# A third bank in the output projection, values of the second block by 7 products, and attention moved to the borders between groups

## The chip, the cores and the metric

One core of a Trainium2 chip. The metric is device time in microseconds (us) of one execution; lower is better. Executions of one kernel in one session agree within a few tenths of a per cent (0.7 at most here, in head_only). The experiments ran on three chips; each timed ratio compares a kernel with the one before on the same chip in the same rounds, while traces are compared across chips. The time of a run is mostly about 1.8 us longer than the span of its cores; both are quoted, and never mixed in one difference.

## The reference

Eight batches of attention with keys and values projected to 64 rows, then one gated feed-forward layer over all 8192 tokens:

```python
k_proj = np.einsum('ks,bhsd->bhkd', E, k)          # 8 batches, 8 heads, 1024 x 64
v_proj = np.einsum('ks,bhsd->bhkd', F, v)
scores = np.matmul(q, k_proj.transpose(0, 1, 3, 2)) / np.sqrt(64)
attn = exp(scores - max); attn /= attn.sum(-1)     # shortened
x = np.matmul(attn, v_proj)                        # then 8192 tokens x 512
gate = 1.0 / (1.0 + np.exp(-(x @ w_gate)))         # 512 -> 1536
val = x @ w_val
return (gate * val) @ w_out                        # 1536 -> 512
```

## The kernel before

The tokens go in 16 blocks of 512, two to a batch. In a block TensorE makes 12 gate tiles (4 matmuls of 128x512 each), 12 value tiles and an output projection, and between these the attention of the next batch. From the third block on, the values are made by 7 products of half-size matrices in place of 8 (a Strassen-type scheme: sums of inputs and of weights are formed on VectorE first, and products are combined in the banks of PSUM, the memory that matmuls write, and by adds afterwards). Matmuls then have 256 columns, and 28 of them replace 16 of 512. From the second block on, the output projection works in the same way. The first two blocks take their values plainly:

```python
for blk in (0, 1):
    todo.append(lambda blk=blk: first_pair(blk, None if blk else lambda: xo(1)))
    for m in range(2, NF):
        todo.append(lambda blk=blk, m=m: mstep(blk, m))    # 4 gate + 4 value matmuls, 512 columns
for tt in range(4):
    todo.append(lambda tt=tt: oproj(0, tt, ffn.next()))
# ... attention(1) hung on slots 12 to 22, weight sums on slot 13
```

One group of four value tiles by 7 products. `A11` to `A22` are quarters of the input, `B11` to `B22` of the weights, `S` and `T` sums of them. TensorE takes a gate tile between any two of these pieces; `v_snap` is a copy on ScalarE, `v_add` and `hidden` run on VectorE:

```python
def p1():
    held_v["a"] = a = FF.take()
    v_product(blk, q, a, "A11", "B11", start=True)              # product 1
    v_snap(0, a)
def p26():
    a = held_v["a"]
    held_v["c"] = c = FF.take()
    v_product(blk, q, c, "A12", "B21", start=True, stop=True)   # product 2
    v_add(0, c)
    v_product(blk, q, a, "S2", "T2")                            # product 6, needs weight sum 2
    v_snap(1, a)
    hidden(K, 0, 0, vsnap[0][:, :], [("vsnap", 0)])
def p57():
    a, c = held_v["a"], held_v["c"]
    v_product(blk, q, c, "S1", "T1", start=True)                # product 5, needs v_add(0) done
    v_product(blk, q, a, "S3", "T3")
    v_snap(2, a)
    v_add(2, c)
# ... p4 (A22 T4) and p3 (S4 B22) finish the group
```

The output projection, cut to the order that matters; `keep_snap` runs on ScalarE, `add_snap`, `plus` and `s_sums` on VectorE:

```python
def first_products(blk, hooks={}):
    a, c = AA.two()
    product(blk, a, "A11", "B11", True)
    keep_snap(0, a)
    product(blk, c, "A12", "B21", True, True)
    hooks.get(-1, int)()                        # in the sixth batch a multiplication of the attention
    add_snap(0, c, 0, 0)                        # frees c
    ...
    product(blk, a, "S2", "T2")
    product(blk, c, "S1", "T1", True)           # waits for that add

def final_products(blk):
    ...
    plus(snap[1], [("snap", 1)], 1, c, slice(0, 512))
    product(blk, b, "A12", "B21", True, True)
    add_snap(0, b, 0, 0)
    s_sums(blk, 4, (0, 6))                      # last product waits for this sum
```

Each engine's instructions run in the order of the program text, and the program waits on semaphores where data need it. So a slot in the schedule decides what stands in front of an instruction in its engine's queue.

The softmax here doesn't subtract the row's maximum and nothing guards it: scores larger than these inputs give would overflow.

## Time and profile before

| | before |
|---|---|
| time, median of the first three runs (range) | 533.45 us (533.1 to 534.06) |
| span of the trace | 531.77 us |
| first gate tile of the first block starts | 21.10 us |
| first gate tile of the second block ("the border") | 45.46 us |
| first product of the second block's projection | 87.00 us |
| from there to the end | 444.77 us |

In the lines of the profile PE is TensorE, PEld its weight loads, DVE VectorE, ACT ScalarE, POOL GpSimd and SP SyncE.

The change adds three groups, in a stretch where the engines are used like this (columns: stretch and length, busy time and count of TensorE, weight loads, VectorE, ScalarE, GpSimd, clock, DMA share, GB/s):

```profile
45.00:87.00 42.00, 41.07 (x267) 17.77 (x270) 27.32 (x44) 20.05 (x38) 3.65 (x4) 1.00 1.21 197
```

VectorE is idle for a third of this stretch (27.3 of 42 us), which is what invites the change.

### The profile page before, as it was taken

The numbers are of one execution on the slowest core, as the hardware profiler recorded it, in microseconds if no ns is written. First come the engines' busy times: TensorE is split into PE (matmuls) and PEld (weight loads), VectorE is DVE, ScalarE is ACT, GpSimd is POOL, SyncE is SP. The second block draws the span as 40 slices with busy tenths as digits, with TensorE's granted clock in tenths as the row PEclk, the third lists the DMA queues.
The fourth block names the chain that finished last, engine by engine and source line by source line (L and its number), as shares of the span: only waits on it lengthen the run. The fifth ranks groups of instructions, "written<-read, shape, count | busy, mean of one in ns | idle before, by whom it ended". The sixth has DMA issues, their size and how long they took to land.

```text
span 531.8 us, 10315 instructions
## 1 busy us (share of the span) xinstructions
PE 515.8 (97%) x4074; PEld 347.1 (65%) x4137; DVE 407.9 (77%) x662; ACT 302.8 (57%) x544; POOL 133.6 (25%) x148
## 2 busy tenths in 40 slices
PE   4999999999999999999999999999999999999997
PEld 4544446656857667585766767676685867777676
DVE  3645386888987788877988679887888788897855
ACT  2654733588385574846568474764838564554541
POOL 9310200105800085001930048100650009200000
DMA  9999999893294254911689224962520020202022
GB/s 158 200 198 203 164 201 217 144 192 75 37 222 78 81 92 66 235 40 61 91 145 173 80 46 48 209 109 80 92 80 1 1 82 3 79 2 80 1 80 80
DMA packets 77152, 56.18 MB, mean 106 GB/s; under 512 B 34800, under 2 KB 69296, under 8 KB 77104
## 3 DMA queue, kind: packets, MB, share of 16 engines
q0 software_dynamic: 33984, 29.89, 36.4%
q1 hardware_dynamic: 43120, 25.63, 19.7%
q8 instruction: 32, 0.52, 0.4%
q14 instruction: 16, 0.13, 0.1%
HBM read 60.29 MB, written 16.78 MB: 145 GB/s over the span
## 4 chain that ended last, share of the span: by engine, by line
PE 91%; DMA 4%; DVE 3%; issue 1%; POOL 1%; ACT 0%; DVEq 0%; ACTq 0%; POOLq 0%
PE pF L264 60%; PE pA L264 30%; DMA KVs<-in_v_dram 2%; DMA qT<-Qb 2%; DVE xT L952 1%; DVE hT L1153 0%; DVE rden L844 0%; POOL KVs L282 0%; POOL Qb L282 0%; DVE ost L1283 0%; DVE vsnap L1489 0%; DVE xT L691 0%; DVE rden L639 0%; DVE hT L1231 0%; DVE EF L1353 0%
## 5 line engine op out<-in xcount | busy, mean ns | idle before, releaser
L264 PE MATMUL pF<-xT,wG 128*128 128x512 bf16 x709 | 187.7, 379 | 4.0 <-issue 0.4
L920 POOL PARTITION_BROADCAST KVs<-eT x96 | 97.0, 1037 | 244.6 <-PE pF L264 191.8
L268 ACT ACTIVATE sig<-pF 128x512 f32<-128x512 f32 x192 | 115.5, 602 | 52.9 <-PE pF L264 50.9
L1489 DVE TENSOR_TENSOR vsnap<-pF,vsnap 128x512 f32<-128x512 f32 x126 | 86.8, 689 | 38.5 <-PE pF L264 28.8
L264 PEld LDWEIGHTS pF<-xT,wG 128*128 128x128 bf16 x768 | 73.7, 98 | 57.6 <-issue 1.7
L268 ACT ACTIVATE vsnap<-pF 128x512 f32<-128x512 f32 x126 | 75.3, 598 | 45.0 <-PE pF L264 42.3
L1470 DVE SCALAR_TENSOR_TENSOR hT<-sig,vsnap 128x512 bf16<-128x512 f32 x126 | 87.3, 693 | 6.2 <-ACT vsnap L268 0.5
L264 PE MATMUL pF<-xT,wV 128*128 128x256 bf16 (+1 forms) x429 | 75.4, 296 | 0.2
L264 PE MATMUL pA<-wO,hT 128*128 128x256 bf16 x534 | 63.4, 273 | 0.4 <-DVE hT L1231 0.4
L264 PEld LDWEIGHTS pF<-xT,wV 128*128 128x128 bf16 x432 | 40.7, 98 | 27.7 <-issue 5.3
L264 PEld LDWEIGHTS pA<-wO,hT 128*128 128x128 bf16 x534 | 52.2, 98 | 7.0 <-DVE hT L1231 0.7
L264 PE MATMUL pF<-xS,wV 128*128 128x256 bf16 x336 | 50.5, 273 | 0.3 <-DVE vsnap L1489 0.2
L264 PE MATMUL pF<-xS,vT 128*128 128x256 bf16 x336 | 50.4, 273 | 0.0
L952 DVE TENSOR_TENSOR xT<-xu,KVs 128x512 bf16<-128x512 f32 x48 | 47.4, 1023 | 1.2 <-POOL KVs L920 0.7
L264 PEld LDWEIGHTS pF<-xS,wV 128*128 128x128 bf16 x336 | 32.2, 98 | 23.7 <-DVE vsnap L1489 3.9
L268 ACT ACTIVATE EF<-pA 128x512 f32<-128x512 f32 x30 | 17.9, 597 | 47.9 <-PE pA L264 47.9
L264 PE MATMUL pA<-wT,hT 128*128 128x256 bf16 x360 | 44.2, 273 | 0.0
L264 PE MATMUL pA<-wT,hS 128*128 128x256 bf16 x360 | 41.9, 273 | 0.6 <-DVE ost L1283 0.6
L264 PEld LDWEIGHTS pA<-wT,hT 128*128 128x128 bf16 x360 | 35.2, 98 | 7.1
L264 PEld LDWEIGHTS pA<-wT,hS 128*128 128x128 bf16 x360 | 35.1, 98 | 4.9 <-DVE ost L1283 0.9
L264 PEld LDWEIGHTS pF<-xS,vT 128*128 128x128 bf16 x336 | 32.9, 98 | 3.8
L1283 DVE SCALAR_TENSOR_TENSOR ost<-pA,EF 128x512 f32<-128x512 f32 x29 | 20.0, 689 | 19.3 <-PE pA L264 19.1
(112 smaller groups left out, 487.7 us busy)
## 6 DMA issues: line engine op xcount, KB each, us to landing
out_dram<-ost SPq DMA_DIRECT2D x60, 256.0 KB, 2.4
Qb<-in_q_dram POOLq DMA_DIRECT2D x7, 1024.0 KB, 20.2
KVs<-in_k_dram POOLq DMA_DIRECT2D x7, 1024.0 KB, 12.6
KVs<-in_v_dram POOLq DMA_DIRECT2D x7, 1024.0 KB, 16.4
wO<-in_moe_w_out_dram POOLq DMA_DIRECT2D x1, 1536.0 KB, 12.3
wG<-in_moe_w_gate_dram POOLq DMA_DIRECT2D x5, 256.0 KB, 18.5
wV<-in_moe_w_val_dram POOLq DMA_DIRECT2D x5, 256.0 KB, 19.0
KVs<-in_k_dram POOLq DMA_DIRECT2D x2, 512.0 KB, 8.4
```

Source lines behind the costliest of these rows:

```text
L264: return add("PE", lambda e: e.matmul(o, lhsT, rhs, **kw), r=r, x=[("bank", b)])
L268: return add("ACT", lambda e: e.activation(o, i, func, scale=scale), r=r, w=w, x=x)
L920: lambda e, n=n, i=2 * rnd + c, j=j, parts=parts: e.partition_broadcast(rb[0:parts, n, :], rrow[32 * j : 32 * j + 1, i, :], channels=parts),
L952: lambda e: e.tensor_tensor(xT[s][:, r, :, 256 * g : 256 * g + 256], xu[:, n, :].rearrange("p (f c) -> p f c", f=2), y.rearrange("p (f c) ...
L1283: lambda e: e.scalar_tensor_tensor(o, bank[bk][:, :].rearrange("p (j c) -> p j c", j=2), 0.5, snap[n].rearrange("p (j c) -> p j c", j=2), ...
L1470: lambda e: e.scalar_tensor_tensor(o, sg[:, :, cc], 1.0, x.rearrange("p (j c) -> p j c", j=2), ALU.add, ALU.mult,),
L1489: lambda e: e.tensor_tensor(o, bank[bk][:, :], o, ALU.add),
```

## The change

The intent is to take columns off TensorE (the second block's values by 7 products in place of 8) and to remove waits (a third PSUM bank in the projection, so that no product waits for the first add; an earlier sum in the last block). To make room, the second batch's attention moves to the borders between groups, the first batch's second half moves one tile earlier, and a few constants move to other memory so that the weight sums can be written sooner. The diff, cut to its core:

```diff
 def first_products(blk, hooks={}):
-    a, c = AA.two()
+    a, c, d = AA.take(), AA.take(), AA.take()
     ...
-    product(blk, c, "A12", "B21", True, True)
+    product(blk, d, "A12", "B21", True, True)
     hooks.get(-1, int)()
-    add_snap(0, c, 0, 0)
+    add_snap(0, d, 0, 0)
+    AA.append(d)
 # --- final_products
-    plus(snap[1], [("snap", 1)], 1, c, slice(0, 512))
     product(blk, b, "A12", "B21", True, True)
+    s_sums(blk, 4, (0, 6))
     add_snap(0, b, 0, 0)
-    s_sums(blk, 4, (0, 6))
+    plus(snap[1], [("snap", 1)], 1, c, slice(0, 512))
 # --- the schedule of the first two blocks
-put(13, lambda: (vt_sums(3), vt_sums(2)))
+put(9, lambda: vt_sums(3))
+put(9, x_sums(1, 1, 2))
+put(10, lambda: (vt_sums(2), vt_sums(1)))
+for u in range(3):                              # second block: three groups of 7 products
+    pieces, p3 = quad_pieces(3 + u, u < 2)
+    todo += [last_piece] + pieces
+    last_piece = p3
+on(0, 1, x_sums(1, 3, 4))
+on(0, 2, lambda: vt_sums(4))
+on(0, 6, n1["k_alone"])                         # attention of the second batch
+on(1, 4, n1["v_alone"])
+for u, name in ((2, "scores"), (3, "mixed")):
+    on(u, 0, n1[name])
 ...
```

`on(u, j, ...)` hangs work behind piece j of group u, `put(i, ...)` behind tile i.

More of the change, by code (lines that the diff above doesn't have):

```diff
@@ L144, in bass_linformer_attn__then__ffn_glu_sigmoid_kernel @@
         vT = sbuf("vT", [P, 3, 2, DFF // 2], BF16)
-        early = vT[:, :, :, :].rearrange("p a b c -> p (a b c)")
+        wT = sbuf("wT", [P, 4, NF // 2, 256], BF16)
+        early = [vT[:, :, :, :].rearrange("p a b c -> p (a b c)")]
         used = [0]
@@ L154, in within @@
                 n *= 2
-            t = early[:, used[0] : used[0] + n]
+            t = early[0][:, used[0] : used[0] + n]
             used[0] += n
@@ L168, in bass_linformer_attn__then__ffn_glu_sigmoid_kernel @@
         bsel8f = within([P, 4, 2, 64], FP32)
-        used[0] = 2 * DFF
+        early[0], used[0] = wT[:, :, :, :].rearrange("p a b c -> p (a b c)"), 0
         bsel8 = within([P, 4, 2, 64], BF16)
@@ L210, in bass_linformer_attn__then__ffn_glu_sigmoid_kernel @@
         ost = sbuf("ost", [P, 4, DM], FP32)
-        wT = sbuf("wT", [P, 4, NF // 2, 256], BF16)
         hS = sbuf("hS", [P, 2, NF // 2, 256], BF16)
@@ L805, in k_alone @@
             def k_alone():
-                bk = att.next()
+                bk = AA.take()
                 project(0, 0, [bk, bk], 0)
                 keep_k(bk, 0)
+                AA.append(bk)
             def v_alone():
-                bk = att.next()
+                bk = AA.take()
+                turn_k(Ring((bk,)))
+                AA.append(bk)
+                bk = AA.take()
                 project(1, 1, [bk, bk], 0)
                 keep_v([bk, bk], 0, ["ACT"] * 4)
+                AA.append(bk)
             def sc_one(r, bks):
@@ L885, in bc @@
             def bc(rnd):
-                bks = [att.next() for _ in range(4)]
+                bks = [AA.take() for _ in range(4)]
                 for half_ in range(2):
@@ L900, in bc @@
                     mul(n // 2, n % 2, bks[j])
+                    AA.append(bks[j])
             def gather():
@@ L971, in two @@
                 return [ring.next(), ring.next()]
-            def scores():
-                f, a0, a1 = two(ffn), two(att), two(att)
-                order = (0, 1, 2)
-                for r, bks in zip(order, (f, a0, a1)):
-                    sc_one(r, bks)
-                exp_one(order[0], f)
-                exp_one(order[1], a0)
-                held["sc"] = a1
-            def mixed():
-                f, a0, a1 = two(ffn), two(att), two(att)
-                sc_one(3, f)
-                xo_one(0, a0)
-                xo_one(1, a1)
-                exp_one(3, f)
-                keep_x(0, a0)
-                held["x"] = a1
-            def outputs():
-                f, a0 = two(ffn), two(att)
-                xo_one(2, f)
-                xo_one(3, a0)
-                held["x"] = a0
-                den8(att.next())
-                keep_x(2, f)
-                rec(0)
-            if b == 1:
-                return [
-                    k_alone,
-                    lambda: (turn_k(att), v_alone()),
-                    scores,
-                    lambda: exp_one(2, held["sc"]),
-                    mixed,
-                    lambda: keep_x(1, held["x"]),
-                    outputs,
-                    lambda: rec(1),
-                    lambda: (keep_x(3, held["x"]), split()),
-                    lambda: bc(0),
-                    lambda: bc(1),
-                ]
             def exp_half(r, g, bks):
@@ L1063, in outputs3 @@
                 xo_one(3, a0)
+                if b == 1:
+                    for g in range(2):
+                        x_half(2, g, f)
+                        FF.append(f[g])
+                    for g in range(2):
+                        x_half(3, g, a0)
+                        AA.append(a0[g])
+                    rec(0)
+                    rec(1)
+                    AA.append(bd)
+                    split()
+                    return
                 if b + 1 < B:
@@ L1094, in attention @@
                 mul=mul,
+                k_alone=k_alone,
+                v_alone=v_alone,
+                bc=bc,
             )
@@ L1214, in t_sums @@
             )[n]
-            dve(lambda e: e.tensor_tensor(T[n], a, b, op), r, [("wT", n)])
+            w = [("wT", n)]
+            if n == 0:
+                w += ["bsel8", ("kp", 0), ("kp", 1)]
+                w += [(k, R) for k in ("rhi", "rhl") for R in range(2)]
+            dve(lambda e: e.tensor_tensor(T[n], a, b, op), r, w)
         def s_sums(blk, n, ms, eng="DVE"):
@@ L1365, in final_products @@
             keep_snap(1, a)
+            product(blk, b, "A12", "B21", True, True)
+            s_sums(blk, 4, (0, 6))
+            add_snap(0, b, 0, 0)
             plus(snap[1], [("snap", 1)], 1, c, slice(0, 512))
-            product(blk, b, "A12", "B21", True, True)
-            add_snap(0, b, 0, 0)
-            s_sums(blk, 4, (0, 6))
             product(blk, a, "A21", "T3")
@@ L1400, in vt_sums @@
                 w += ["bsel8f", "identf", "count", "pats"]
-            if n == 4:
-                w += ["bsel8", ("kp", 0), ("kp", 1)]
-                w += [(k, R) for k in ("rhi", "rhl") for R in range(2)]
             r = [("wV", j, x) for j in range(6) for x in range(2)]
@@ L1620, in put @@
             at.setdefault(i, []).append(fn)
-        for blk in (0, 1):
-            todo.append(lambda blk=blk: first_pair(blk, None if blk else lambda: xo(1)))
-            for m in range(2, NF):
-                todo.append(lambda blk=blk, m=m: mstep(blk, m))
-        for tt in range(4):
-            todo.append(lambda tt=tt: oproj(0, tt, ffn.next()))
-        qt2, sc2, den2, bc2, xo2 = half_unit(1, att)
-        put(4, lambda: (qt2(0, ("DVE", "ACT")), qt2(1, ("DVE", "ACT"))))
-        put(5, lambda: (sc2(0), sc2(1)))
@@ L1631, in bass_linformer_attn__then__ffn_glu_sigmoid_kernel, with h_sums @@
-        put(5, second_loads)
-        put(7, lambda: (den2(), xo2(0), xo2(1)))
-        late = []
-        def spread2():
-            now = bc2(0)
-            late.append(bc2(1))
-            now()
-        put(9, spread2)
-        put(10, lambda: late[0]())
-        for i, fn in zip((12, 14, 15, 16, 17, 18, 19, 19, 20, 21, 22), attention(1)):
-            put(i, fn)
-        put(16, lambda: (load_k(2), load_v(2), load_q(2)))
-        put(25, transpose_q)
+        def h_sums(blk, ms, *ns):
+            return lambda: [s_sums(blk, n, ms) for n in ns]
@@ new lines, in x_sums @@
+        def x_sums(blk, *ns):
+            return lambda: [xs_sums(blk, n) for n in ns]
+        A, Z = (0, 4), (4, 6)
+        todo.append(lambda: first_pair(0, lambda: xo(1)))
+        for m in range(2, NF):
+            todo.append(lambda m=m: mstep(0, m))
+        qt2, sc2, den2, bc2, xo2 = half_unit(1, att)
+        put(3, lambda: (qt2(0, ("DVE", "ACT")), qt2(1, ("DVE", "ACT"))))
+        put(4, lambda: (sc2(0), sc2(1)))
+        put(4, second_loads)
+        put(6, lambda: (den2(), xo2(0), xo2(1)))
@@ new lines, in bass_linformer_attn__then__ffn_glu_sigmoid_kernel, with own_banks, quad_pieces @@
+        put(8, lambda: (bc2(0)(), bc2(1)()))
+        put(9, lambda: vt_sums(3))
+        put(9, x_sums(1, 1, 2))
+        put(10, lambda: (vt_sums(2), vt_sums(1)))
+        def own_banks():
+            FF[:] = [ffn.next() for _ in range(4)]
+            AA[:] = [att.next() for _ in range(4)]
+        put(10, own_banks)
+        last_piece = lambda: g_step(3, 0)
+        def quad_pieces(K, more):
+            p1, p26, p57, p4, p3 = v_pieces(K)
+            return [
+                p1,
+                lambda: g_step(K, 1),
+                p26,
+                lambda: g_step(K, 2),
+                p57,
+                lambda: g_step(K, 3),
+                p4,
+                (lambda: g_step(K + 1, 0)) if more else (lambda: None),
+            ], p3
@@ new lines, in bass_linformer_attn__then__ffn_glu_sigmoid_kernel, with on @@
+        for u in range(3):
+            pieces, p3 = quad_pieces(3 + u, u < 2)
+            todo += [last_piece] + pieces
+            last_piece = p3
+        todo.append(last_piece)
+        last_piece = lambda: g_step(6, 0)
+        def on(u, j, fn):
+            put(11 + 9 * u + j, fn)
+        on(0, 1, x_sums(1, 3, 4))
+        on(0, 2, lambda: vt_sums(4))
+        n1 = attention(1)
+        late1 = n1["late"]
+        on(0, 6, n1["k_alone"])
+        on(1, 4, n1["v_alone"])
+        on(1, 6, lambda: (load_k(2), load_v(2), load_q(2)))
@@ new lines, in bass_linformer_attn__then__ffn_glu_sigmoid_kernel @@
+        for u, name in ((2, "scores"), (3, "mixed")):
+            on(u, 0, n1[name])
+            if u == 2:
+                on(u, 1, lambda: late1("A0", 0))
+                on(u, 3, lambda: late1("A0", 1))
+                on(u, 6, lambda: (late1("A1", 0), late1("A1", 1)))
+            else:
+                on(u, 0, lambda: [late1(x, g) for x in ("A0", "A1") for g in range(2)])
+        on(2, 0, h_sums(1, A, 1))
+        on(2, 4, h_sums(1, A, 2, 3))
+        on(3, 0, h_sums(1, Z, 1, 2, 3))
@@ L1647, in kv2 @@
+        for tt in range(4):
+            todo.append(lambda tt=tt: oproj(0, tt, FF.take()))
+        on(3, 1, n1["outputs"])
+        on(3, 2, lambda: n1["bc"](0))
+        on(3, 2, lambda: t_sums(2))
+        on(3, 3, lambda: n1["bc"](1))
+        on(3, 3, lambda: (t_sums(0), t_sums(1)))
         def kv2():
-            bk = att.next()
+            bk = AA.take()
             kv(2, bk)
@@ L1652, in kv2 @@
             vd_one(bk, 1)
-        put(24, kv2)
-        put(13, lambda: (vt_sums(3), vt_sums(2)))
-        put(20, lambda: s_sums(1, 1, (0, 3)))
-        put(21, lambda: (s_sums(1, 2, (0, 3)), s_sums(1, 3, (0, 3))))
-        put(22, lambda: [s_sums(1, n, (3, 6)) for n in (1, 2, 3)])
-        put(23, lambda: t_sums(0))
-        put(24, lambda: (t_sums(1), t_sums(2)))
-        put(25, lambda: t_sums(3))
+            AA.append(bk)
+        on(3, 4, kv2)
+        on(3, 4, lambda: t_sums(3))
+        on(3, 4, transpose_q)
         for i, slot in enumerate(todo):
@@ L1666, in bass_linformer_attn__then__ffn_glu_sigmoid_kernel @@
         assert not at
-        FF[:] = [ffn.next() for _ in range(4)]
-        AA[:] = [att.next() for _ in range(4)]
-        last_piece = lambda: g_step(6, 0)
         for b in range(1, B):
@@ L1675, in bass_linformer_attn__then__ffn_glu_sigmoid_kernel @@
                 K = 6 * b + u
-                p1, p26, p57, p4, p3 = v_pieces(K)
-                todo += [
-                    last_piece,
-                    p1,
-                    lambda K=K: g_step(K, 1),
-                    p26,
-                    lambda K=K: g_step(K, 2),
-                    p57,
-                    lambda K=K: g_step(K, 3),
-                    p4,
-                    (lambda K=K: g_step(K + 1, 0)) if K + 1 < 6 * B else (lambda: None),
-                ]
+                pieces, p3 = quad_pieces(K, K + 1 < 6 * B)
+                todo += [last_piece] + pieces
                 last_piece = p3
@@ L1691, in on @@
                 put(9 * u + j, fn)
-            def h_sums(blk, ms, *ns):
-                return lambda: [s_sums(blk, n, ms) for n in ns]
-            def x_sums(blk, *ns):
-                return lambda: [xs_sums(blk, n) for n in ns]
-            A, Z = (0, 4), (4, 6)
             o0, o1 = 2 * b - 1, 2 * b
             if b == 1:
-                first = {1: lambda: (vt_sums(1), vt_sums(4), x_sums(2, 1, 2, 3, 4)())}
+                first = {1: x_sums(2, 1, 2, 3, 4)}
                 on(0, 0, lambda: first_products(o0, first))
```

## The prediction

> **What bounds the kernel now.** I read the page first, then the chain of work that ended last in order of time, then the timeline of single engines in the stretches that the diff touches.
>
> The page says which engine carries the time:
>
> ```profile
> PE 515.8 (97%) x4074; PEld 347.1 (65%) x4137; DVE 407.9 (77%) x662; ACT 302.8 (57%) x544; POOL 133.6 (25%) x148
> ...
> PE 91%; DMA 4%; DVE 3%; issue 1%; POOL 1%; ACT 0%; DVEq 0%; ACTq 0%; POOLq 0%
> ```
>
> TensorE is busy 97% of the span and is 91% of the chain. So time leaves this kernel in two ways only: fewer columns through TensorE, or less waiting of TensorE. There are about 16 us outside PE's busy time, a third of them before anything can be multiplied. The diff's third bank aims at waits, its 7 products at columns.
>
> The chain shows where PE hands over to another engine:
>
> ```profile
> 445.53 2.63 PE pA L264 x24
> 448.25 1.15 DVE xT L952
> 449.40 0.61 DVE ost L1283
> 450.06 2.79 PE pA L264 x24
> ...
> 523.49 0.68 DVE EF L1353
> 524.34 0.48 issue
> 524.82 0.96 DVE hT L1231
> 525.83 2.14 PE pA L264 x18
> ```
>
> In the steady batches the output projection stands in the chain as unbroken runs of 60 matmuls in 6.55 us, 0.109 us each: no wait there. Only two places are broken. At 448 us a multiplication by the broadcast denominators (L952) sits ahead of the add that frees the projection's second bank, and PE starts 0.76 us late (24 matmuls from 445.37 should end at 447.99 + 12 x 0.109 = 449.30, and the next starts at 450.06). At the end PE waits 0.61 us (12 x 0.109 after 523.91 is 525.22, next start 525.83) for the sum written over hT, which is queued behind two other VectorE instructions.
>
> The border of the first two blocks, by engine:
>
> ```profile
> 43.34 0.42 PE L264 MATMUL pA<-vT 32*128 32x128 bf16 x16
> 43.70 1.04 PE L264 MATMUL pF<-xT,wG 128*128 128x512 bf16 x4
> 44.57 1.03 PE L264 MATMUL pF<-xT,wV 128*128 128x512 bf16 x4
> 45.46 1.04 PE L264 MATMUL pF<-xT,wG 128*128 128x512 bf16 x4
> 46.33 1.03 PE L264 MATMUL pF<-xT,wV 128*128 128x512 bf16 x4
> 47.65 0.39 PE L264 MATMUL pF<-xT,wG 128*128 128x512 bf16 x1 [0.29 <-DVE xT L691]
> ```
>
> ```profile
> 44.12 1.28 DVE L691 TENSOR_TENSOR xT<-pA,xu 128x512 bf16<-128x512 f32 x2
> 45.70 0.69 DVE L1153 SCALAR_TENSOR_TENSOR hT<-sig,pF 128x512 bf16<-128x512 f32 x1 [0.30 <-PE pF L264]
> ...
> 94.99 0.95 DVE L1412 TENSOR_TENSOR wV<-wV 128x1536 bf16<-128x1536 bf16 x1
> 95.85 0.95 DVE L1412 TENSOR_TENSOR vT<-wV,vT 128x1536 bf16<-128x1536 bf16 x1
> 96.72 0.42 DVE L1432 TENSOR_TENSOR xS<-xT 128x512 bf16<-128x512 bf16 x1
> 97.17 0.42 DVE L1432 TENSOR_TENSOR xS<-xS,xT 128x512 bf16<-128x512 bf16 x1
> ```
>
> Four 512-column matmuls take 0.87 us from start to start. The second block starts at 45.46 and PE loses 0.45 us at 47.65, waiting for the second half of x. On VectorE the distance between starts is what counts: 0.61 us for an instruction on a bank of 512 fp32, 0.87 for a weight sum of 1536 bf16, 0.34 for a sum of 512 bf16 (0.45 when it needs the one before it).
>
> **What the Trainium skill says.** "TensorE: Matmul & The Clock Gate", section "Wait — 56ns, not 53.3ns?": once warm, start to start is N columns at 2.4 GHz plus some 2.5 ns. The trace agrees: 0.216 us for 512 columns, 0.109 for 256 (2.62 us for 24), at a granted clock of 1.00. "Perfetto Trace Analysis", section "Tensor Engine Instruction (MATMUL, LD_WEIGHTS)": VectorE and ScalarE are strict FIFO, TensorE's end is estimated. So I count from starts, and an early-placed sum holds up everything behind it; the break at 448 us is such a case. "VectorE: DVE Perf Modes", section "What auto-detection actually checks": a two-source op doubles its rate only if all is 16-bit. The trace agrees: 0.95 us for 1536 bf16 against 0.69 for 512 out of an fp32 bank.
>
> **The change part by part.**
>
> Columns. The second block's values take 12 x 4 matmuls of 512 columns, 48 x 0.216 = 10.37 us. By 7 products they are 3 groups x 28 matmuls of 256, 84 x 0.109 = 9.16 us. Saved on PE: 1.2 us. This is on the path.
>
> Old waits removed at the start. From 45.46 to the second block's output projection at 87.00 are 41.54 us. Pure work is 10.37 for gates, 10.37 for values, 10.37 for the first block's projection, 0.86 for one more gate, and 7.6 for the second batch's attention (k 0.99, its turning 0.39, v 1.06, scores 0.8, mixed 0.77, outputs 1.11, spreading 0.66, next batch's k and v 1.84): 39.6. So some 1.95 us of it are waits: 0.45 at the border, 0.3 for the transposed q (landing at 59.77, scores started at 59.04), 0.3 for banks in the spreading, the rest small. In the new order the scores come later and the first two go away.
>
> New waits at the start. This is where I expect the gain to go. The order of instructions of the changed kernel puts on VectorE, from the gate of tile 9 to the first add of the second block: gate, 4 scalings, gate of tile 10, weight sum 3, x sums 1 and 2, gate of tile 11, weight sums 2 and 1, x sums 3 and 4, weight sum 4, add. PE ends tile 9 at about 41.66 (half attention moved one tile earlier, the rest only permuted), so VectorE starts at 41.93 and runs without a gap: 0.61 + 2.43 + 0.61 + 0.87 + 0.80 + 0.61 + 0.87 + 0.87 + 0.68 + 0.87 = 9.2 us, then the add until 51.8. PE meanwhile: tiles 10 and 11 end at 45.5, gate 46.34, product 1 46.78, gate 47.64. Product 2 needs the bank of tile 11 (freed 47.93): 0.35 late. Product 6 needs weight sum 2 (48.80): 0.43 late. Gate until 50.16. Product 5 needs the bank that the add frees: 51.88, 1.7 late. Together 2.5 us on the path.
>
> Then: the 4 copies of v (1.6 us on ScalarE in the trace) come just ahead of the snapshot that product 4 waits for, about 0.6 us; the mixed step has no gate tile between the last products and itself, so it waits for two exponentials, about 0.5; the second spreading waits for its banks as now, 0.4; small ones 0.2. New waits 4.2 against 1.95 old: +2.25, with the 1.2 saved makes the start about 1.05 us longer.
>
> Second batch. Its VectorE queue loses two weight sums (1.9 us), and the 0.32 us that PE waits at 99.53 go: -0.3.
>
> Third bank. Only the break at 448 us is freed, 0.76 us. VectorE is busy 27.6 of 30 us there and still waits for GpSimd's broadcasts, so the next add (starting 457.42, done 458.1, with PE at 458.35) will hold PE for some 0.35. Net -0.4.
>
> End. The sum over hT starts right after its product, 524.18 in place of 524.82, and is done by 525.13, before PE needs it. Then the product after next waits for a snapshot (525.42 + 0.60, plus 0.06), so PE gets 0.4 of the 0.61.
>
> Sum: +1.05 - 0.3 - 0.4 - 0.4 = -0.05 us.
>
> **The rivals.** First, PE's columns decide and the sums are hidden: then the start gains 1.2 plus up to 0.75 of old waits, and all parts sum to about -3 us, 530.4. For it speaks that VectorE is idle in half of 43 to 60 us; against it, that the sums all sit in the first ten of these. Second, the mixing of attention with 7 products makes ScalarE a bound as well (7 evacuations per group, 4.2 us of 6.5, with 8 exponentials and 8 copies put between): then the start loses 3 us or more, 535.5. Against it: the same mixture runs in the steady batches with waits of about 0.1 us. Third, loads: a start of the attention one tile earlier meets q's second half, which lands at 29.49 and 30.82 with the transposes at 30.3: 0.15 us at most. The output weights land at 69.99 and are first used at about 73 in either kernel; were they later, that wait would be new.
>
> **Range and chances.** The sum says 533.4. Each new wait is counted from a queue that I am sure of in order, but with durations of other stretches, and orders that are tuned tend to be somewhat better than such a count; I take 533.1. The first rival in part gives 531.6, the second in part 534.6. 2% are 10.7 us, more than all the parts together: within 2% is near certain.
>
> **What would show it.** PE's matmuls on wV and vT in the second block at 0.109 us; a wait of PE for the vsnap add of about 1.7 us near 50 to 52 us, and two smaller ones before it; the second block's first projection product starting near 88.1, not 87.0; unbroken 60 matmuls in the sixth batch, with a new wait of some 0.35 us on the vsnap add 8 us later; the last wait of PE 0.15 in place of 0.61. I am wrong if the first projection product starts before 86.5 (sums hidden) or after 89.5 (ScalarE or a load).

## More of the kernel before

The prediction shows the lines on which it rests. Three groups of the page and one stretch are worth reading beside them. A group line has line, engine, operation, tiles, shapes and count, then the busy time, the mean nanoseconds of one, and the idle time of that engine just before:

```profile
L1489 DVE TENSOR_TENSOR vsnap<-pF,vsnap 128x512 f32<-128x512 f32 x126 | 86.8, 689 | 38.5 <-PE pF L264 28.8
...
L268 ACT ACTIVATE vsnap<-pF 128x512 f32<-128x512 f32 x126 | 75.3, 598 | 45.0 <-PE pF L264 42.3
L1470 DVE SCALAR_TENSOR_TENSOR hT<-sig,vsnap 128x512 bf16<-128x512 f32 x126 | 87.3, 693 | 6.2 <-ACT vsnap L268 0.5
```

These three are the price of a group of 7 products outside TensorE: 126 is 42 groups of 3, so each group adds three adds on VectorE, three copies on ScalarE, and gate multiplications that read the copies.

## The result, and the profile after

| | before | changed | changed − before |
|---|---|---|---|
| time, median (range), 4 runs each on one chip | 533.36 (533.10 to 534.06) | 533.87 (533.79 to 533.98) | ratio 1.0008, 95% interval 0.999 to 1.0025: the same |
| span of the trace | 531.77 | 531.99 | +0.22 |
| first gate | 21.10 | 20.92 | −0.18 |
| border | 45.46 | 45.47 | +0.01 |
| first product of the second block's projection | 87.00 | 88.06 | +1.06 |
| last product of that projection begins | 96.16 | 97.37 | +1.21 |
| steady batches, up to the projection at 446 us | 445.37 | 446.25 | +0.88 |
| behind the projection of the sixth batch | 455.30 | 455.59 | +0.29 |
| some 20 us later | 474.87 | 475.48 | +0.61 |
| at the last block's old wait | 525.83 | 525.84 | +0.01 |

Ratios here and below are the mean time of one kernel's fast runs over that of the other's of the same rounds, so they are not quite the ratio of the medians quoted beside them. The rows below the border are starts of the same TensorE instruction in both traces. They read as an account: the start costs 1.2 us, three other places give back 0.33, 0.59 and 0.60 us, one takes 0.32 again, and a last wait takes 0.2. What is left is 0.22 us of span, less than the timed runs can show.

The first part of the page of the changed kernel, and the engines of its chain:

```profile
PE 519.6 (98%) x4173; PEld 351.1 (66%) x4173; DVE 415.0 (78%) x675; ACT 307.7 (58%) x553; POOL 133.5 (25%) x148
...
PE 93%; DMA 2%; DVE 2%; POOL 1%; ACT 1%; issue 1%; DVEq 0%; POOLq 0%
```

The busy time of TensorE rises although it has fewer columns to make. Two things of the record do this: the trace has 4173 matmul records, as many as weight loads, where that before has 63 fewer than weight loads; and a matmul's modelled end outlasts its issue, so that more and shorter matmuls with gaps behind them show more busy time. Starts are the safe reading: four matmuls of 256 columns take 0.44 us from start to start (46.33 to 46.77), four of 512 take 0.87.

TensorE of the changed kernel behind the border (start, busy time, instruction, count; in brackets the idle time and what ended it):

```profile
46.77 1.03 PE L264 MATMUL pF<-xT,wG 128*128 128x512 bf16 x4
47.82 0.61 PE L264 MATMUL pF<-xT,wV 128*128 128x256 bf16 x4
48.69 0.61 PE L264 MATMUL pF<-xS,vT 128*128 128x256 bf16 x4 [0.26 <-DVE vT L1394]
49.13 1.03 PE L264 MATMUL pF<-xT,wG 128*128 128x512 bf16 x4
51.70 0.61 PE L264 MATMUL pF<-xS,wV 128*128 128x256 bf16 x4 [1.53 <-DVE vsnap L1471]
...
63.02 0.61 PE L264 MATMUL pF<-xT,vT 128*128 128x256 bf16 x4 [0.48 <-ACT vsnap L268]
...
88.06 2.78 PE L264 MATMUL pA<-wO,hT 128*128 128x256 bf16 x24
90.83 2.78 PE L264 MATMUL pA<-wT,hS 128*128 128x256 bf16 x24
```

The bracket counts from the modelled end of the matmul before; from the time at which the next could have started it is 0.17 us more. So the waits are 0.19 us at 47.82 (46.77 + 0.87 = 47.64 would have been free), 0.42 at 48.69, 1.70 at 51.70 and 0.65 at 63.02. And this is the queue of VectorE that makes the third of them:

```profile
47.68 0.95 DVE L1394 TENSOR_TENSOR vT<-vT,wV 128x1536 bf16<-128x1536 bf16 x1
48.55 0.95 DVE L1394 TENSOR_TENSOR wV<-wV 128x1536 bf16<-128x1536 bf16 x1
49.42 0.42 DVE L1414 TENSOR_TENSOR xS<-xT 128x512 bf16<-128x512 bf16 x1
49.75 0.42 DVE L1414 TENSOR_TENSOR xS<-xT,xS 128x512 bf16<-128x512 bf16 x1
50.09 0.95 DVE L1394 TENSOR_TENSOR vT<-wV,vT 128x1536 bf16<-128x1536 bf16 x1
50.95 0.68 DVE L1471 TENSOR_TENSOR vsnap<-pF,vsnap 128x512 f32<-128x512 f32 x1
```

No line has an idle bracket: VectorE goes from sum to sum without a gap, and the add that frees product 5's bank (the last line) is behind all of them. Its operands were there earlier: product 2 was started at 47.82. Its end, 51.64, and the start of product 5, 51.70, are one event.

The same stretch by engines, again up to the first product of the projection:

```profile
45.00:88.00 43.00, 40.59 (x307) 21.10 (x306) 34.94 (x56) 23.66 (x45) 3.64 (x4) 1.00 1.15 187
```

VectorE has 7.6 us more to do and ScalarE 3.6 us more, TensorE 0.5 us less, and the stretch takes 1 us longer. By average shares no engine but TensorE is near its limit.

Near the end, the chain of waits of the changed kernel:

```profile
446.41 6.55 PE pA L264 x60
...
455.59 1.48 PE pA L264 x12
...
519.45 7.21 PE pA L264 x66
...
526.69 1.49 PE pA L264 x12
```

The 60 matmuls are whole now: the two VectorE lines that broke them at 448 us are gone. At two of these starts a wait remains: 0.19 us at 455.59 (in the timeline the 12 matmuls before it start at 454.10, and 454.10 + 12 x 0.109 = 455.40) and 0.20 us at 526.69, in place of the 0.61 a microsecond before.

### The profile page after: what moved, and what is told of

Its sections match the earlier page's. It is cut to its first block, busy times and chain, and to the rows that moved or that the text cites. A ratio compares the mean times of both kernels' runs of the same rounds, so it can differ in the third digit from the quotient of the medians.

```text
span 532.0 us, 10476 instructions
## 1 busy us (share of the span) xinstructions
PE 519.6 (98%) x4173; PEld 351.1 (66%) x4173; DVE 415.0 (78%) x675; ACT 307.7 (58%) x553; POOL 133.5 (25%) x148
## 4 chain that ended last, share of the span: by engine, by line
PE 93%; DMA 2%; DVE 2%; POOL 1%; ACT 1%; issue 1%; DVEq 0%; POOLq 0%
PE pF L264 62%; PE pA L264 32%; DMA KVs<-in_v_dram 2%; DVE vT L1394 0%; DVE hT L1133 0%; DVE vsnap L1471 0%; ACT vsnap L268 0%; POOL KVs L282 0%; DVE xT L691 0%; ACT vpD L268 0%; POOL Qb L282 0%; DVE xS L1414 0%; DVE rden L639 0%; DVE ost L1338 0%; POOL quad L356 0%
## 5 line engine op out<-in xcount | busy, mean ns | idle before, releaser
L264 PE MATMUL pF<-xT,wG 128*128 128x512 bf16 x768 | 197.5, 379 | 0.3
L1471 DVE TENSOR_TENSOR vsnap<-pF,vsnap 128x512 f32<-128x512 f32 x135 | 92.9, 688 | 44.3 <-PE pF L264 31.0
L268 ACT ACTIVATE vsnap<-pF 128x512 f32<-128x512 f32 x135 | 80.7, 598 | 49.0 <-PE pF L264 46.0
L1452 DVE SCALAR_TENSOR_TENSOR hT<-sig,vsnap 128x512 bf16<-128x512 f32 x135 | 93.5, 693 | 6.2
L264 PE MATMUL pF<-xT,wV 128*128 128x256 bf16 (+1 forms) x408 | 66.9, 286 | 0.0
L264 PE MATMUL pF<-xS,wV 128*128 128x256 bf16 x360 | 54.1, 273 | 1.8 <-DVE vsnap L1471 1.5
L264 PE MATMUL pF<-xS,vT 128*128 128x256 bf16 x360 | 54.0, 273 | 0.3 <-DVE vT L1394 0.3
L264 PEld LDWEIGHTS pF<-xT,wV 128*128 128x128 bf16 x408 | 38.2, 98 | 24.0 <-issue 5.7
L264 PEld LDWEIGHTS pF<-xS,wV 128*128 128x128 bf16 x360 | 34.3, 98 | 27.2 <-DVE vsnap L1471 6.5
L264 PEld LDWEIGHTS pF<-xS,vT 128*128 128x128 bf16 x360 | 35.2, 98 | 4.6 <-DVE vT L1394 0.5
```

The costliest lines, as they stand in the source:

```text
L264: return add("PE", lambda e: e.matmul(o, lhsT, rhs, **kw), r=r, x=[("bank", b)])
L268: return add("ACT", lambda e: e.activation(o, i, func, scale=scale), r=r, w=w, x=x)
L1452: lambda e: e.scalar_tensor_tensor(o, sg[:, :, cc], 1.0, x.rearrange("p (j c) -> p j c", j=2), ALU.add, ALU.mult,),
L1471: lambda e: e.tensor_tensor(o, bank[bk][:, :], o, ALU.add),
```

## The experiments

Starts vary from run to run by more than what is measured here. The first gate tile began between 20.86 and 22.61 us in the traces below, with the same instructions ahead of it in all kernels that have the new start. The chain of work ahead of it leads back to loads of the first batch (of v in head_only and best2, of k in extra_ahead). So a trace is read from one milestone to the next ("border to projection": from the second block's first gate tile to the first product of its projection; "projection to end": from there on), and the timed runs are quoted beside it.

| kernel | border to projection | projection to end | span |
|---|---|---|---|
| before | 41.54 | 444.77 | 531.77 |
| changed | 42.59 | 443.93 | 531.99 |
| third_bank | 41.03 | 444.51 | 532.06 |
| end_order | 41.02 | 444.36 | 531.49 |
| head_only | 42.59 | 444.56 | 534.22 |
| early_sums | 40.26 | 443.92 | 530.23 |
| extra_ahead | 43.48 | 443.94 | 534.36 |
| extra_behind | 42.60 | 443.96 | 533.29 |
| v_on_vector | 41.94 | 446.05 | 534.46 |
| best | 40.12 | 444.01 | 529.35 |
| best2 | 39.60 | 443.91 | 529.21 |
| best3 | 45.61 | 444.66 | 535.88 |
| early_paced | 40.26 | 443.96 | 529.64 |

The theory under test is the prediction's: the start is longer because the new sums stand ahead of the add in VectorE's queue, and three small gains elsewhere pay for it. The rivals are that the cost comes from the number of products itself (ScalarE's copies, or TensorE's shorter matmuls), and that the time is set by the loads. All eleven kernels of these experiments gave correct results.

One thing in this table was not asked for. Between the border and the projection, third_bank and end_order are the kernel before, instruction for instruction, and take 41.03 and 41.02 us where its own trace took 41.54. The difference lies in two places of that trace: 0.34 us at the scores, for the transposed q that landed at 59.77 us, and 0.17 us behind the turning of k, for v, which landed at 56.17 us and was used at 56.21. In the other two traces the border came later, at 46.52 and 46.11 us; v landed at about the same time (56.31 and 56.16), and this piece of q a microsecond sooner (58.79 and 58.53), so both were there. So the old start can lose half a microsecond to loads, when it begins early or when they land late. The new one asks for q later, and does not: 42.59, 42.59 and 42.60 us for borders at 45.47, 47.06 and 46.73. With the loads in place the new start costs 1.57 us, not 1.05.

### The three parts alone

The third bank alone (the first hunk of the diff above, put into the kernel before):

> The kernel before with the third bank alone. If the bank frees only the one break in the sixth batch: that wait of 0.76 us goes, two VectorE waits of 0.2 and 0.3 us appear within 10 us after it, the span is 0.2 to 0.4 us shorter, all other stretches keep their times within 0.05 us. Rival, the bank helps in every batch: the span falls by more than 1 us.

Measured: 533.68 us (532.9 to 534.32, 5 runs) against 533.5 (532.39 to 534.13, 11 runs); ratio 1.0008, interval 0.9994 to 1.0022. From projection to end it is 0.26 us shorter in the trace. The chain shows unbroken 60 matmuls and a new break behind them:

```profile
446.07 6.55 PE pA L264 x60
...
455.26 1.48 PE pA L264 x12
```

So the wait of 0.76 us at 448 us is gone, and 0.5 us of it comes back as short waits within the next 20 us. In the timed runs a quarter of a microsecond can't be told from nothing.

The order in the last block alone (the second hunk):

> The kernel before with the new order of the last products' VectorE work alone. If the snapshot on ScalarE takes over half of the wait: TensorE's wait before the last A12 product (0.6 us) goes, one of 0.2 us appears before the A22 product, the span is 0.4 us shorter. Rival, the closing stores decide the end: the span stays within 0.1 us although the last matmul starts 0.4 us earlier.

Measured: 533.33 us (532.54 to 533.9, 6 runs) against the same 533.5; ratio 1.0004, interval 0.999 to 1.0019. In the trace it takes 0.41 us off the part behind the first projection, with the wait of 0.61 gone and one of 0.20 in its place:

```profile
518.94 7.21 PE pA L264 x66
...
526.18 1.48 PE pA L264 x12
```

The new start alone (the changed kernel with both hunks undone):

> The changed kernel with third bank and last order undone: the second block's 7 products and the moved attention alone. Theory: this part alone is slower than before by 0.7 to 1.0 us of span (the second block's first projection product starts at about 88.05, 1.06 us later, and 0.2 to 0.3 come back in the second batch). Rival, the bank's new rotation makes the start longer: then the start is shorter here than in the changed kernel.

Measured: 535.28 us (534.12 to 537.74, 6 runs), ratio 1.0043, interval 1.0023 to 1.0063. Border to projection is 42.59 us, the same hundredth as in the changed kernel, and the rest is 0.21 us shorter than before (the waits at 99.5 us that the second batch loses, less some small ones). By these two figures it should be 0.84 us above the kernel before, or 1.36 with the 41.02 us of end_order's trace for the old start. The runs show 2.3 (0.0043 x 533.5). Its profiled run began its first gate tile 1.2 us later than the kernel before, after a wait for v, and met one of 0.18 us for q at 32.36 us, which the kernel before doesn't have; its border came 1.6 us later. That explains the profiled run; for the other five it is not shown, and some 0.9 us of the timed difference stay open. In the traces the parts add up from the border on: +1.05 − 0.21 − 0.26 − 0.41 = +0.17, and the changed kernel shows +0.21 there.

### Is it the queue of VectorE?

First, put less ahead of the add. Two weight sums go to earlier tiles, where VectorE has gaps, and the two last sums go behind the add:

```diff
-put(9, lambda: vt_sums(3))
+put(6, lambda: vt_sums(3))
+put(7, lambda: vt_sums(2))
 put(9, x_sums(1, 1, 2))
-put(10, lambda: (vt_sums(2), vt_sums(1)))
+put(10, lambda: vt_sums(1))
-on(0, 1, x_sums(1, 3, 4))
-on(0, 2, lambda: vt_sums(4))
+on(0, 1, x_sums(1, 3))
+on(0, 3, x_sums(1, 4))
+on(0, 3, lambda: vt_sums(4))
```

> The changed kernel with weight sums 3 and 2 ahead of the scalings, in VectorE's idle time, and x sum 4 and weight sum 4 behind the second block's first add. If the FIFO of VectorE is the cause: the waits of 0.19, 0.42 and 1.70 us at 47.6 to 51.7 us go, the first projection product starts at about 85.8, the span falls by 2.0 to 2.4 us against the changed kernel and by 1.8 to 2.2 against the one before. Rival, the mixing with attention or ScalarE holds TensorE anyway: the three waits turn into others and less than 0.8 us is gained.

Its TensorE behind the border:

```profile
48.22 0.60 PE L264 MATMUL pF<-xT,wV 128*128 128x256 bf16 x4
48.65 0.60 PE L264 MATMUL pF<-xS,vT 128*128 128x256 bf16 x4
49.09 1.03 PE L264 MATMUL pF<-xT,wG 128*128 128x512 bf16 x4
49.95 0.60 PE L264 MATMUL pF<-xS,wV 128*128 128x256 bf16 x4
```

No bracket is left: each piece starts when the one before it lets it. Border to projection falls from 42.59 to 40.26 us, by 2.33; the three waits were 2.31. The same sums, products and copies are made, in another order, so the number of products was not what cost. The span fell by 1.76 us against the changed kernel, not by 2.0 to 2.4, since this run began its first gate tile 0.58 us later. The timed runs gained less over the kernel before (the changed kernel was not in these rounds): 532.9 us (531.12 to 533.37, 6 runs), ratio to the kernel before 0.9992, interval 0.9977 to 1.0008. The profiled run, with its span of 530.2 us, was the second shortest of the six, whose spans went up to 531.6. Two things can make the gain over the kernel before smaller in other executions. Against an old start with its loads in place, 41.02 us, the stretch is 0.76 us shorter and not 1.28. And, a suspicion only, the output weights may come late: in this trace they landed at 70.33 us and were first used at 70.84, half a microsecond later.

Second, put more ahead of it, and the same behind it. A sum of 1536 bf16 a partition that nobody needs there (it is made again later) is worth 0.87 us of VectorE:

```diff
-on(0, 2, lambda: vt_sums(4))
+on(0, 2, lambda: (vt_sums(4), s_sums(0, 1, (0, 6))))     # extra_ahead
+on(0, 3, lambda: s_sums(0, 1, (0, 6)))                   # extra_behind, with vt_sums(4) as it was
```

> The changed kernel with one sum more of 1536 elements on VectorE (a result nobody reads), right behind weight sum 4 and so ahead of the second block's first add. If VectorE's queue ahead of that add is on the path: TensorE's wait of 1.70 us grows to 2.57 (0.87 more, the distance of two such sums), and the stretch from the block border to the first projection product goes from 42.59 to 43.45 us. Rival, the sum of VectorE's work over the stretch matters, or other waits absorb it: clearly less.

> The same extra sum, but behind that add and its gate product, where VectorE has 0.97 us idle. If only the place in the queue matters: the wait stays at 1.70 us and the stretch at 42.59, within 0.1. Rival, VectorE's total work matters: the same growth as with the sum ahead.

Measured, one look each: 536.28 us and 535.08 us. These single times tell nothing between such kernels; the traces do. First of extra_ahead, then of extra_behind:

```profile
54.04 0.61 PE L264 MATMUL pF<-xS,wV 128*128 128x256 bf16 x4 [2.40 <-DVE vsnap L1471]
```

```profile
52.96 0.61 PE L264 MATMUL pF<-xS,wV 128*128 128x256 bf16 x4 [1.54 <-DVE vsnap L1471]
```

The same work costs TensorE 0.87 us when it stands ahead of the add (2.57 against 1.70, and 43.48 against 42.59 us of border to projection) and 0.01 us when it stands right behind it. So the place in VectorE's queue, and not the amount of its work, makes the start's largest wait.

### The fourth wait: copies on ScalarE

The four copies of the second batch's v move from ScalarE, where they stand ahead of the snapshot at 62.37 us, to VectorE:

```diff
-keep_v([bk, bk], 0, ["ACT"] * 4)
+keep_v([bk, bk], 0, ["DVE"] * 4)
```

> The changed kernel with the four copies of the second batch's v on VectorE (idle for 3.2 us there) in place of ScalarE. If ScalarE's queue made the wait of 0.65 us before the second group's product 4: that wait goes, nothing takes its place, the stretch from border to projection is 41.9 to 42.0 us in place of 42.59. Rival, the copies are slower on VectorE and hold its add: at least 0.3 us of wait remain.

In the trace the wait of 0.65 us is gone and border to projection is 0.65 us shorter (41.94):

```profile
63.38 0.60 PE L264 MATMUL pF<-xT,vT 128*128 128x256 bf16 x4
```

The timed runs don't follow: 534.22 us (534.02 to 536.26, 4 runs), ratio 1.0019 to the kernel before, interval 1.0004 to 1.0035. The profiled run (the one of 536.26) began its first gate 1.2 us later than the changed kernel, and its span ended 5.43 us after its last matmul began, not 3.43 as in the changed kernel, with last stores that took 2 us longer to land. So the stretch is shown to be shorter, and a shorter time of this kernel is not.

### A version with all of it

The kernel "best" has early_sums, v_on_vector, one of two copies of the third batch's v moved behind the first products (the 0.15 us at 90.83, below), and the multiplications of the sixth batch put on other hooks (for the waits that the third bank left):

```diff
 def kv2():
     ...
     vd_one(bk, 0)
-    vd_one(bk, 1)
-    AA.append(bk)
+    kv2_bank.append(bk)        # vd_one(bk, 1) and AA.append behind the first products
 # --- sixth batch
-0: lambda: (mul(1, 0), mul(1, 1), mul(2, 0)),
-1: lambda: (mul(2, 1), mul(3, 0)),
+0: lambda: (mul(1, 0), mul(1, 1)),
+1: lambda: (mul(2, 0), mul(2, 1)),
+   on(5, 3, lambda: mul(3, 0))
```

> Early sums, the copies of v on VectorE, one copy of the third batch's v moved behind the first projection products, and in the sixth batch two multiplications moved behind the adds. Waits that should go against the changed kernel: 0.19 + 0.42 + 1.70 at the block border, 0.65 before product 4, 0.15 in the projection, 0.3 to 0.5 in the sixth batch. Stretch from border to projection 39.6 us, from projection to the end 443.4 us; time 2.0 to 3.5 us under the kernel before, 0.4 to 0.65 per cent.

Measured: 532.26 us (531.15 to 533.72, 6 runs) against 533.63; ratio 0.9977, interval 0.9964 to 0.999. That is a gain of 1.2 us, less than the 2.0 to 3.5 expected, and both stretches came out longer than expected (40.12 and 444.01). The multiplications gained nothing: there were waits of 0.30 us at 459.04 and 0.31 at 462.83 in place of the old ones. And a new wait shows up, by a transfer:

```profile
69.88 2.75 PE L264 MATMUL pF<-wO,hT 128*128 128x512 bf16 x12 [0.47 <-DMA wO<-in_moe_w_out_dram]
```

The output weights landed at 69.75 us, and TensorE would have used them 0.53 us before it did (in best2 below, 0.67 us lie between the matmuls on eT and these; here it is 1.20). The expectation for best2 puts this wait at 0.65; that counts in the wait of 0.12 us for an exponential just before. The load's start is paced by the program: it is not begun before the first two pieces of transposed q have landed. So this pace was varied, with the multiplications back in their old places: released by one piece ("best2"), and not held back at all ("best3").

```diff
-    r=turned()[:2],            # as in the changed kernel
+    r=turned()[:1],            # best2
+    r=[],                      # best3
```

> As the best so far, without the moved multiplications of the sixth batch (they made two waits of 0.3 us and gained nothing), and with the load of the output weights released by the first transposed q instead of the first two. If pacing alone made the new wait of 0.65 us before the first output projection: the weights land 0.3 to 0.8 us earlier, that wait is under 0.3 us, border to projection 39.5 to 39.8 us, projection to end 443.8; time 0.4 to 0.6 per cent under the kernel before. Rival, the queue of loads sets the landing: wait and stretch stay at 0.65 and 40.1.

> The same with no pacing of that load at all. If the transposes of q have 3 us to spare before the scores: the weights land 2 to 5 us earlier, the wait is gone and nothing else moves, border to projection 39.5 us. Rival, the load takes the transposes' bandwidth: the transposed q lands after 61 us and the scores wait for it.

best2: 531.31 us (530.44 to 532.21, 6 runs) against 533.73 (532.75 to 534.66, 11 runs); ratio 0.9952, interval 0.9938 to 0.9965. That is about half a per cent less than the kernel before, well clear of noise though under the 2% from which a verdict here would say faster. The changed kernel was not in these rounds; its own ratio of 1.0008 puts it behind best2 as well. The weights landed at 67.34 us, 2.4 us sooner and not 0.3 to 0.8, and were used at 69.82, without a wait. best3: 538.92 us (537.62 to 540.54, 4 runs), ratio 1.0097. The transposes issued between 40 and 72 us, of best2 first, then of best3 (the last column is the median of the microseconds from issue to landing):

```profile
qT<-Qb SPq DMA_TRANSPOSE x4, 10.2
```

```profile
qT<-Qb SPq DMA_TRANSPOSE x4, 13.6
```

and TensorE of best3:

```profile
61.48 0.60 PE L264 MATMUL pF<-xS,wV 128*128 128x256 bf16 x4
66.64 0.64 PE L264 MATMUL pF<-qT,kpD 64*64 64x512 bf16 x4 [4.55 <-DMA qT<-Qb]
```

With the load of the weights in flight from 34.66 us on (from 55.48 in best2), the transposes of q landed late (the third and fourth at 66.50 and 67.39 us, at 59.17 and 59.95 in best2), and the scores waited 4.6 us for them. The weights themselves landed no more than 1.4 us sooner (65.97).

The stretch is 6.0 us longer than in best2, though, not 4.6. The rest is the clock. Two stretches of best3, the second behind the wait (the third number from the end is the granted clock):

```profile
60.00:62.00 2.00, 2.00 (x14) 1.09 (x12) 1.97 (x4) 1.03 (x3) 0.00 (x0) 1.00 1.23 195
66.60:68.00 1.40, 1.36 (x12) 0.43 (x12) 0.00 (x0) 0.66 (x2) 0.00 (x0) 0.50 0.16 32
```

In this trace the granted clock is at half from 66.18 to 69.59 us, after TensorE had stood still since 61.9; matmuls of 256 columns there start 0.213 us apart, and from the scores to the projection it takes 24.58 us, not 23.20 as in best2. So there is a pace that is too late by half a microsecond, and one so early that it costs six.

The last run puts the pace of best2 to early_sums, to see whether the weights had held back that kernel's timed runs:

> Early sums again, with the load of the output weights released by the first transposed q. The profiled run of early sums was its fastest of six; the others were some 1.8 us slower. If in those the output weights landed too late for the first output projection (in the profiled run they landed 0.5 us ahead of it): the six runs here move to 531 to 532.3 us, ratio 0.996 to 0.9975, with the stretch from border to projection at 40.26 in the profile. Rival, the spread comes from the first loads at the start: the times stay near 532.9, ratio 0.999, spread over 2 us.

Measured: 532.24 us (531.44 to 532.32, 5 runs) against 533.32; ratio 0.9976, interval 0.9963 to 0.999. Border to projection is 40.26 us, as in early_sums, with the weights landing at 68.10 and used at 70.20. The stretch is the same and the time better (ratio 0.9976 after 0.9992, with intervals that overlap), which agrees with late weights in the executions of early_sums that were not traced. It is not shown: the two kernels ran on different chips, and the expectation starts from a slip. The profiled run of early_sums was its second shortest by span (530.2 us, the others 529.3 and 531.0 to 531.6), but only its fourth fastest by time (532.96).

## Why the prediction was right

The predicted time was 533.1 us, the measured 533.87, inside the range of 531.6 to 534.6, and within 2% as said. A small gain was predicted and a small loss measured, within noise (+0.4 us, interval −0.5 to +1.3), so the sign is not shown. What was right is the mechanism: a start that VectorE's queue makes longer, about paid for by three small gains. The steps, in the prediction's order:

- **The start, "about 1.05 us longer".** It was 1.05 against the trace from which the prediction was made (42.59 for 41.54), but 1.57 against two later traces of the same old start; the old waits of "some 1.95 us" held 0.51 us for loads, which the two later traces don't show. The first product of the projection was put near 88.1 and came at 88.06. The steps inside it: "0.35 late" for product 2 was 0.19, "0.43 late" for product 6 was 0.42, "1.7 late" for product 5 was 1.70; together 2.31 for the predicted 2.5. The snapshot behind the four copies of v ("about 0.6") was 0.65. The mixed step's wait for exponentials ("about 0.5") was 0.12, at 72.25. Just before it, at 71.14, 0.28 us passed that the prediction does not name: the third group's last product waited for the vsnap add. The spreading ("0.4") showed 0.20 (the second took 0.54 us where the first took 0.33). The named waits make 3.28 us for the predicted 4.0 without "small ones", with the unnamed one 3.56; since the total is right, some 0.6 us must lie in gaps too small to name or in the old waits, which the prediction took as a remainder. That these errors cancel to a hundredth is luck. early_sums, extra_ahead, extra_behind and v_on_vector show the cause of 2.31 + 0.65 of it; the rest is read from one trace.
- **Second batch, "−0.3".** It was −0.33; the wait at 99.53 us is gone.
- **An omission.** Between the two, the prediction has nothing, and the runs show +0.15: the product at 90.83 us needs the first snapshot's bank, and ScalarE takes that snapshot at 90.09 only, behind three copies for the third batch and a gate. Before, these copies were done earlier:

```profile
87.33 1.02 ACT L268 ACTIVATE kpd<-pA 64x1024 bf16<-64x1024 f32 x1 [8.96 <-PE pA L264]
88.37 1.21 ACT L268 ACTIVATE vpD<-pA 64x512 bf16<-64x512 f32 x2
89.60 0.60 ACT L268 ACTIVATE sig<-pF 128x512 f32<-128x512 f32 x1
90.09 0.59 ACT L268 ACTIVATE EF<-pA 128x512 f32<-128x512 f32 x1
```

- **Third bank, "net −0.4".** The mechanism held: the break of 0.76 us went and a part came back. The part was mis-sized. "Some 0.35" at one place was 0.19, 0.13 and 0.19 at three (455.59, 458.78 and 465.49), 0.5 in all, so the net was −0.26 in third_bank alone and −0.27 in the changed kernel (by the milestones −0.59 + 0.32; the first of the three lies ahead of the milestone at 455.59).
- **End, "PE gets 0.4 of the 0.61".** It got 0.41 in end_order alone and 0.40 in the changed kernel (−0.60, then a new wait of 0.20).
- **The sum, "−0.05 us".** It is +0.22 in the traces. The omission (+0.15) and the third bank (+0.13) account for it. Against the old start with its loads in place it would be half a microsecond more, which the timed ratio of 1.0008 (0.4 us, interval −0.5 to +1.3) can neither show nor exclude.
- **From the sum to 533.1.** The sum said 533.4; the prediction then took off 0.3 since "orders that are tuned tend to be somewhat better than such a count". No view of the profile stood behind that step, and it was wrong: the time was above the count, not below it.

Of the rivals, the first (sums hidden, 530.4) was not what the changed kernel does, though early_sums shows that it only takes another order to hide them: its start is 1.28 us shorter than that of the kernel before in the trace that was predicted from, 0.76 us with loads in place. The second, ScalarE as a bound, is true of three single waits (0.65, 0.15 and 0.12 us), not of the stretch. The third, loads, did not touch the changed kernel, and came up as soon as the start was shorter (best).

## What to carry to other kernels

An engine that is idle for a third of a stretch is no free place for new work: what counts is what stands ahead of the one instruction for which the critical engine waits. Here 0.87 us of work ahead of an add cost 0.87 us, and behind it nothing. So when work is added to an in-order queue, start it as early as its inputs allow or put it behind the next instruction that frees a buffer, and after each gain look at the loads that were paced for the old time. And a long wait of TensorE can cost more than its length: in best3 4.6 us of waiting cost 6.0, since the granted clock was at half for 3.4 us of what followed.

## What the Trainium skill lacked or had wrong

- "Perfetto Trace Analysis", section "DVE / Act Engine Instruction (TENSOR_ADD, Activation, etc)", draws the spread of the semaphore update behind the end that the profiler reports, but that section gives it no duration. These traces show TensorE starting 0.04 to 0.06 us after that end where it waited for nothing else (VectorE 51.64 to 51.70, ScalarE 62.98 to 63.02).
- "DMA: Bandwidth & Descriptors", section "Rules for kernel authors", says that a transpose next to ordinary DMAs needs nothing. That is said of correctness, and best3 was correct; but it does not say what the transpose loses in time. Beside an unpaced load of 1.5 MB, the fourth transposed piece of q landed at 67.39 us, not 59.95, and TensorE waited 4.6 us.
- No page gives the spread of the first loads from run to run. With the same instructions ahead of it, the first gate tile started between 20.86 and 22.61 us in the traces of the ten kernels with the new start, a spread of 1.75 us, which is more than any of the three parts of this change is worth.
